# An attention-and-experts kernel: the order of all engines written out anew over cycles of four pairs

## The chip, the cores and the metric

The kernel runs on one core of one Trainium2 chip. The metric is the device time of one execution in microseconds. The engines of a core are named as in the profile: PE is the matmul array (TensorE), PEld its weight loads, DVE the vector engine, ACT the scalar engine, POOL the GpSimd engine, SP the engine whose queue issues most transfers. Each engine works through its own queue in order and waits on semaphores for the others.

## What is computed

A decaying causal attention over 8 batches x 8 heads x 576 positions of 64 values, whose output of 4608 rows of 512 goes through a mixture of 8 experts with the single best expert for each row:

```
scores = q @ k.T / 8
cum    = cumsum(log(clip(f, 1e-4, 1)))
scores = where(causal, -1e9, scores + cum[i] - cum[j])
attn   = softmax(scores);  x = attn @ v          # x: rows of 8 heads x 64
e      = argmax(x @ w_gate);  g = softmax(x @ w_gate)[e]
out    = g * (relu(x @ w1[e]) @ w2[e])           # w1: 512 x 1024, w2: 1024 x 512
```

All is float32. The term cum[i] is the same for a whole row and drops out of the softmax, so the kernel adds only -cum[j] (times 8, as the scores are scaled later).

## The kernel before

**Pairs.** Two heads make a pair, four pairs a batch, 32 pairs in all. In a pair the first 512 queries are cut into tiles t = 0 to 3 of 128 rows; tile t needs 128 (t + 1) keys. The last 64 queries of two neighbouring pairs are put together into one joint tile J, which is done with the even pair. For a pair n the steps are:

- `s_mm` (words S1, S2, S3): scores of t = 1, of t = 2 and 0, of t = 3, for head j = 0 and 1, each head into its own PSUM bank. `j_mm` (J0, J1): the two halves of the joint tile.
- `red` (r and t and j: `r10` is t = 1, j = 0) and `j_red` (q): one DVE instruction adds the decay tile, writes the scores to SBUF and gives the row's minimum (the signs are turned). `ex` (x) and `j_ex` (y): the exp on ACT with the row's sum.
- One pair later: transposes of the probabilities on PE into a bank (TA to TE for the tiles, TF to TH for J), each followed by a copy to SBUF on ACT or DVE (`cAs` is the copy of TA on ACT, `cBv` that of TB on DVE).
- Two pairs later: `av` (V0: queries 320 to 575, V1: 0 to 319) multiplies with v, and a copy (`o0s`, `o1v`) takes the result to xT. `j_place` (P) moves the joint tile's second half into place on POOL.

After the four pairs of a batch come its sums (A0 to A2), the gate logits (G, L0, L1, R), five tiles of x that are turned back, scaled on DVE and written to DRAM (F0 to F4, `fin_x`), and ten stages that choose the expert and the place of each row (the letters m e g w k s p h l b; k and b have matmuls).

**Order.** Nothing is scheduled by a program: `InOrder.pin` ties each instruction to the one before it on its engine, in the order in which the code issues it. That order stands in STEPS, a text for each of the four places of a pair in its batch, which `cycle` reads word by word. All four begin with the same words:

```python
SC = "S1 r10 r11 x10 x11 S2 r20 r00 r21 r01 S3 "
SC + """TA cAs TB cBv @0 TC cCs TD cDv @1 TE cEs !!F1 r30 r31 x20 x00 x21 x01 @2
    !!e V0 o0s x30 @3 J0 q00 q01 J1 q10 q11 @4 V1 x31 o1s !A1 !!g y0 y1 @5 @6"""
```

`!` marks a step of the batch before, `!!` of two batches before; `@0` to `@6` are slots in which loads and pieces of expert 0 are put. Pair n's loads stand ahead of its text: the decay tile of pair n + 1 (`load_d`), v of pair n, q and k of pair n + 2. On POOL `masks` copies the decay tile and adds the causal masks. A write of a tile of x to DRAM is put off by three slots (`c.later`).

**PSUM.** Eight banks. One (`ps_r`) serves the routing. Scores and J take turns in four (`ps_4`), transposes, AV and the rest in three (`ps_x`).

**Start.** Warm-up matmuls (`keep_busy`, L253) stand ahead of the first scores, and one in each slot of pairs 0 and 1. For pair 0 the decay comes from TensorE (`sel` and `cum`, a matmul of its own after each score matmul, L386), since the decay tiles are read from DRAM, where `cd` is written first; the mask-only tile `Ws[0]` is zeroed on POOL. Pair 1 and the rest use loaded decay tiles.

**End.** Expert 0 is split into two chunks of rows: the first 384 come from batches 0 to 5 and are known early. Its loads, splits into two float32r parts, first matmuls (`up`) and the turning of its rows are put into slots of the last pairs; `finish` then writes out by hand how the rest of the ups, the downs (`down`) and the routing of the last batch follow each other. Then come the second chunk of expert 0 and the experts 1 to 7, which are the same before and after.

Of the kernel before, what the change touches and what calls it, by code (L numbers as in the profile page):

```python
# [19 lines left out]
P = 128  # L20
S = 576
# [52 lines left out]
def open_pools(c, ctx, tc):  # L74
# [15 lines left out]
    c.ps_4, c.ps_x = Turns(banks[:4]), Turns(banks[4:])  # L90
# [94 lines left out]
def attention_all(c, tc, qkT, va, vb, f, wgd, x_dram, batch_done, more_consts, extra):  # L185
# [11 lines left out]
    with ExitStack() as st:  # L197
# [69 lines left out]
        NW = 9 * P  # L267
        Ws = [ap_.tile([P, 2, NW], F32, name=f"dec{i}") for i in range(2)]
# [4 lines left out]
        sel = ap_.tile([P, P], F32, name="sel")  # L273
        G.memset(sel, 0.0)
        for j in range(2):
            G.memset(sel[j * HD : j * HD + 1], 1.0)
# [13 lines left out]

        def load_d(n):
            sp_dma(Ws[n % 2][:, :, 3 * P : 7 * P],
                   cdv[n : n + 1, :, 0:512].to_broadcast([P, 2, 512]))
# [6 lines left out]
        def masks(n):  # L300
            W = Ws[n % 2]
            blk = W.rearrange("p j (a b) -> p j a b", b=P)
            m = tri.unsqueeze(1).unsqueeze(1).to_broadcast([P, 2, 2, P])
            G.tensor_copy(W[:, :, 0 : 2 * P], W[:, :, 3 * P : 5 * P])  # L304
            G.tensor_tensor(blk[:, :, 7:9], blk[:, :, 3:5], m, ALU.add)
            G.tensor_tensor(blk[:, :, 2:7:4], blk[:, :, 5:7], m, ALU.add)
# [5 lines left out]
        def decay(n, j, t):  # L312
            W = Ws[n % 2][:, j]
# [60 lines left out]
        def s_mm(n, ts):  # L374
            raw = raws[n]
            banks = [psum(c.ps_4) for _ in range(2)]
            o = 0
            for t in ts:
                w = P * (t + 1)
                for j in range(2):  # L380
                    h = slice(j * HD, (j + 1) * HD)
                    r = raw[h]
                    note(nc.tensor.matmul(banks[j][:, o : o + w], r[:, P * t : P * t + P],  # L383
                                          r[:, QW : QW + w], start=True, stop=n > 0))
                    if n == 0:
                        note(nc.tensor.matmul(banks[j][:, o : o + w], sel[h], cum[h, 0:w],  # L386
                                              start=False, stop=True))
                    got[n, j, t] = banks[j][:, o : o + w]
                o += w
# [15 lines left out]
        def j_mm(n, half):  # L405
            banks = [psum(c.ps_4) for _ in range(2)]
# [76 lines left out]
        def av(n, half):  # L483
# [4 lines left out]
            pv = psum(c.ps_x)  # L488
# [31 lines left out]
        def fin_x(b, t, scalar=False):  # L520
# [3 lines left out]
            px = psum(c.ps_s if b == B - 1 and t > 1 else fin_bank[0])  # L524
# [39 lines left out]
        def fin_logits(b, part):  # L564
            rinv = rinvs[b]
            if part == 0:
# [3 lines left out]
            pg = psum(fin_bank[0])  # L570
# [1156 lines left out]
```

## Time and profile before

| | us |
|---|---|
| median of 3 runs | 801.09 (800.36 to 802.25) |
| the profiled execution | 802.73 |
| its span, first to last instruction | 801.0 |
| PE busy in the span | 775.7 (97%) |
| DVE, ACT, POOL busy | 567.0, 496.2, 431.2 |

The span is what the trace shows; the 1.7 us around it belong to the execution's time. Busy times are sums over stages of different kinds. A matmul's end is modelled, so a busy PE is not a PE at its peak.

### The profile page before, as it was taken

To read this page: it belongs to the slowest core of one execution; us is meant where nothing else is said; L and a number is where in the kernel's file an instruction comes from. 1 tells how busy PE (TensorE), PEld (TensorE's weight loads), DVE (VectorE), ACT (ScalarE), POOL (GpSimd) and SP (SyncE) were. 2 spreads that over 40 slices of the span, in tenths; PEclk is the share of its full clock that TensorE was granted. 3 is DMA by queue.
4 is the path that set the end of the run, shared out by engine and by line. 5 is a ranking of instruction groups with operands and counts; after the bars stand their busy time and mean duration, and the time that the engine had idled before them with its cause. 6 is when DMAs were issued, how large, how long until landed. Compare 5 with 4: busy or idle time off the path is not lost.

```text
span 801.0 us, 16552 instructions
## 1 busy us (share of the span) xinstructions
PE 775.7 (97%) x5556; PEld 640.0 (80%) x5556; DVE 567.0 (71%) x1547; ACT 496.2 (62%) x1289; POOL 431.2 (54%) x602
## 2 busy tenths in 40 slices
PE   8999999999999999899999999999999999999996
PEld 6677767676777776688889899898898898998985
DVE  4676888888888888755398848758578488486630
ACT  4788887878778788545366546456365366463521
POOL 5554463636364545681567657546556475475311
PEclk9999999999999999999999999999999999999999
DMA  7987788888788877532345342363343433523300
GB/s 184 206 202 196 183 211 191 205 197 211 186 205 197 212 188 209 180 97 94 114 122 189 106 160 88 106 196 100 115 148 106 153 91 106 162 72 109 111 27 31
DMA packets 83494, 119.54 MB, mean 149 GB/s; under 512 B 9871, under 2 KB 40591, under 8 KB 83408
## 3 DMA queue, kind: packets, MB, share of 16 engines
q1 hardware_dynamic: 76272, 98.38, 46.4%
q0 software_dynamic: 6400, 19.93, 7.5%
q8 instruction: 45, 0.74, 0.4%
q14 instruction: 41, 0.34, 0.2%
q10 hardware_dynamic: 736, 0.16, 0.1%
HBM read 99.25 MB, written 20.22 MB: 149 GB/s over the span
## 4 chain that ended last, share of the span: by engine, by line
PE 84%; DVE 5%; DMA 4%; ACT 2%; issue 2%; POOL 1%; SPq 0%; ACTq 0%; POOLq 0%; DVEq 0%
PE ps L1163 25%; PE ps L1362 17%; PE ps L496 11%; PE ps L383 11%; PE ps L436 10%; PE ps L1133 3%; PE ps L411 2%; PE pr L1362 1%; PE ps L1318 1%; ACT aT L432 1%; DMA dec<-cd 1%; PE ps L557 1%; DMA va_t<-in_va 1%; DVE w1s L1267 1%; ACT row L531 1%
## 5 line engine op out<-in xcount | busy, mean ns | idle before, releaser
L369 ACT ACTIVATE sc<-sc,nmx 128x256 f32<-128x256 f32 (+3 forms) x256 | 141.2, 558 | 8.8 <-DVE nmx L366 8.8
L1163 PE MATMUL ps<-w_0w,hhw 128*128 128x512 f32 x280 | 113.0, 403 | 0.0
L1362 PE MATMUL ps<-X_0w,w1s 128*128 128x320 f32 x504 | 111.9, 309 | 0.0
L1163 PE MATMUL ps<-w_1w,hhw 128*128 128x512 f32 x280 | 110.4, 394 | 0.0
L1163 PE MATMUL ps<-w_0w,hl 128*128 128x512 f32 x280 | 110.1, 393 | 0.0
L496 PE MATMUL ps<-aT,va_t 128*64 128x256 f32 (+3 forms) x896 | 97.2, 358 | 3.9 <-PE ps L436 2.2
L383 PE MATMUL ps<-raw 64*128 64x128 f32 (+3 forms) x512 | 96.6, 457 | 3.1 <-DVE nmj L366 1.8
L496 PEld LDWEIGHTS ps<-aT,va_t 128*64 128x64 f32 x896 | 64.7, 138 | 33.2 <-PE ps L436 4.7
L366 DVE CUSTOM_DVE_ANT_0 sc<-ps,dec 128x384 f32<-128x384 f32 (+1 forms) x192 | 87.9, 508 | 4.3 <-PE ps L383 2.1
L1171 POOL DMA_INDIRECT out<-y,si_fast x37 | 37.4, 1012 | 97.6 <-ACT y L1170 89.1
L1362 PEld LDWEIGHTS ps<-X_0w,w1s 128*128 128x128 f32 x504 | 84.2, 188 | 0.2
L432 ACT COPY aT<-ps 128x256 f32<-128x256 f32 (+2 forms) x144 | 59.1, 448 | 36.6 <-PE ps L436 34.9
L1170 ACT ACTIVATE y<-ps,g_fast 128x512 f32<-128x512 f32 x37 | 25.5, 688 | 87.9 <-PE ps L1163 65.3
L1362 PE MATMUL ps<-X_1w,w1s 128*128 128x320 f32 x252 | 77.7, 308 | 0.0
L430 DVE COPY aT<-ps 128x512 f32<-128x512 f32 (+3 forms) x128 | 60.2, 503 | 19.2 <-PE ps L436 19.0
L304 POOL COPY dec<-dec 128x512 f32<-128x512 f32 x31 | 19.0, 612 | 99.5 <-DMA dec<-cd 94.3
L383 PEld LDWEIGHTS ps<-raw 64*128 64x128 f32 x512 | 56.9, 186 | 19.1 <-DVE nmj L366 2.5
L1163 PEld LDWEIGHTS ps<-w_0w,hl 128*128 128x128 f32 x280 | 52.6, 188 | 12.6
L1163 PEld LDWEIGHTS ps<-w_0w,hhw 128*128 128x128 f32 x280 | 52.5, 187 | 10.8
L1163 PEld LDWEIGHTS ps<-w_1w,hhw 128*128 128x128 f32 x280 | 52.7, 188 | 10.4
L1362 PE MATMUL ps<-xa,w1s 128*128 128x320 f32 x336 | 58.4, 309 | 1.0 <-ACT u L1391 1.0
L1267 DVE TENSOR_TENSOR w1s<-w1r,w1s 128x1024 fp32r<-128x1024 f32 (+1 forms) x42 | 52.8, 1269 | 7.8 <-ACT w1s L1261 7.8
(263 smaller groups left out, 1799.2 us busy)
## 6 DMA issues: line engine op xcount, KB each, us to landing
dec<-cd SPq DMA_DIRECT2D x31, 512.0 KB, 5.6
w1r<-in_w SPq DMA_DIRECT2D x112, 128.0 KB, 3.0
w<-in_w SPq DMA_DIRECT2D x28, 512.0 KB, 4.7
raw<-in_qkT SPq DMA_DIRECT2D x64, 160.0 KB, 5.6
raw<-in_qkT SPq DMA_DIRECT2D x64, 144.0 KB, 5.1
decj<-cd SPq DMA_DIRECT2D x32, 288.0 KB, 4.9
va_t<-in_va SPq DMA_DIRECT2D x32, 256.0 KB, 6.4
x_dram<-row SPq DMA_DIRECT2D x32, 256.0 KB, 3.9
```

The source lines that it names most:

```text
L366: V.tensor_tensor_reduce(dst, src, m, -0.125, init, ALU.add, ALU.min, out)
L369: nc.scalar.activation(x, x, AF.Exp, bias=nmx, scale=-1.0, accum_out=acc)
L383: note(nc.tensor.matmul(banks[j][:, o : o + w], r[:, P * t : P * t + P], r[:, QW : QW + w], start=True, stop=n > 0))
L430: V.tensor_copy(dst, src)
L432: nc.scalar.copy(dst, src)
L436: note(nc.tensor.transpose(out.bitcast(F32R), words, c.identr))
L496: c.last_av = note(nc.tensor.matmul(pv[j * HD : (j + 1) * HD, q0 - qa : qb - qa], l, r, start=(blk == 0), stop=(blk == nb - 1),))
L1163: c.note(nc.tensor.matmul(py, rows(hi_, ft), w[wi], start=(ft + k == 0), stop=(ft == FT - 1 and k == 2),))
L1170: nc.scalar.activation(y, py, AF.Copy, scale=g[:, s : s + 1])
L1171: nc.gpsimd.indirect_dma_start(out=self.out, out_offset=bass.IndirectOffsetOnAxis(ap=si[:, s : s + 1], axis=0), in_=y, in_offset=None, bou ...
L1267: (eng or self.nc.vector).tensor_tensor(lo, raw, hi.bitcast(F32), ALU.subtract)
L1362: self.nc.tensor.matmul(bank[:, 0:HN], w[:, wi, mat, kt], x[xi][:, kt, :], start=start and k == 0, stop=k == 5, skip_group_check=True,)
```

## The change

The order is one text from the first pair to the last: FIRST for pairs 0 to 3, STEPS for a cycle of four pairs (used for pairs 4 to 27), LAST for pairs 28 to 31 and all of expert 0's first chunk. Each word that needs PSUM names its banks (`S2:ta` is the bank t for head 0 and a for head 1), out of seven that all steps share; transposes, AV and scores of neighbouring pairs are mixed more freely, loads (D, DJ, LV, LR), masks (M, MJ) and writes of x (W0 to W4) are words of their own. Copies move between ACT and DVE. Slots, `c.later`, `early_tasks` and `finish` go.

In the start, four warm-up pairs instead of eight and none later; pairs 0 and 1 share the mask-only tile and get their decay by matmuls (words Z, `z_mm`; `sel` holds -8 in one row for each of them, so `cum` is not multiplied by -8 ahead of the scan); pair 1's decay tile is not loaded. The zeroing of `Ws[0]` moves to DVE, the multiplication by -8 for the DRAM copy to POOL.

In the end, w1 loads and splits (`wl`, `ws`), w2 loads and splits (`vl`, `vs`), row fetches and turns (`ef`, `et`, `ee`), ups and downs (`u`, `d`) are words of LAST.

```diff
-    c.ps_4, c.ps_x = Turns(banks[:4]), Turns(banks[4:])
+    c.bank = dict(zip("abcdtvm", banks))
...
-        step(lambda: keep_busy(8))
+        step(lambda: keep_busy(4))
         V.memset(ones, 1.0)
+        NW = 9 * P
+        Ws = [ap_.tile([P, 2, NW], F32, name=f"dec{i}") for i in range(2)]
+        V.memset(Ws[0], 0.0)
         V.tensor_scalar(fr, fr, 1.0e-4, 1.0, ALU.max, ALU.min)
         nc.scalar.activation(fl, fr, AF.Ln)
         pin(nc.scalar.activation(warm, fr[0:1, 0:1], AF.Exp))
-        V.tensor_scalar(fl, fl, -8.0, None, ALU.mult)
         V.tensor_tensor_scan(cum, ones, fl, 0.0, ALU.mult, ALU.add)
-        sp_dma(cd, cum)
...
-        G.memset(Ws[0], 0.0)
-        for j in range(2):
-            for k in (2, 6, 7, 8):
-                G.tensor_copy(Ws[0][:, j, k * P : k * P + P], tri)
+        G.tensor_copy(blocks(Ws[0])[:, :, 7:9], tri4)
+        G.tensor_copy(blocks(Ws[0])[:, :, 2:7:4], tri4)
...
+        G.tensor_scalar(fl, cum, -8.0, None, ALU.mult)
+        sp_dma(cd, fl)
...
+        def dec(n):
+            return Ws[(n + 1) % 2 if n > 1 else 0]
...
+                    note(nc.tensor.matmul(banks[j][:, o : o + w], r[:, P * t : P * t + P],
+                                          r[:, QW : QW + w], start=True, stop=n > 1))
+                    got[n, j, t] = banks[j][:, o : o + w]
+                if n < 2 and len(ts) > 1:
+                    z_mm(n, (t,))
...
+        def z_mm(n, ts):
+            for t in ts:
+                for j in range(2):
+                    h = slice(j * HD, (j + 1) * HD)
+                    note(nc.tensor.matmul(got[n, j, t], sel[h, n], cum[h, 0 : P * (t + 1)],
+                                          start=False, stop=True))
...
         STEPS = [
+            """J0:dt q01 D J1:cb q00 q11 S3:mv A0 y1 LR q10 S2:ta A1 S1:bd r30 V1:c r21 r31 r20 y0
+               r01 r00 r10 x30 r11 e M V0:m o1s TE:a F3:v A2 x00 TA:t x31 o0s TC:c W0 cEs LV cAv
+               F4:d cCs TD:b x01 k cDs x11 s TB:v x10 cBv x21 x20""",
+            """S2:ma r01 S1:bc r00 r10 r20 r21 S3:dt r30 TA:v x00 r31 TG:b D cAs LV p TF:m r11 x20
+               V0:a x31 cFs TH:d cGs TC:t TD:v M DJ o0v cHv cCv LR x30 TB:c F1:m g TE:d cBs l MJ
+               x11 V1:b cEs x21 cDs o1v P x01 x10""",
+            """S3:tm r30 S2:ad r31 D r20 G:bc x30 r01 S1:tm r21 x31 w r00 r11 x20 V1:v r10 J0:ma
+               J1:db TD:t q01 M q00 cDs x00 q11 L1:a TC:c LV q10 y1 F2:m h o1s LR TB:b TE:a cBs
+               TA:t L0:d V0:m cAs y0 x21 o0s cEv x10 cCv x11 W3 x01""",
+            """S1:ta S2:bv r11 R S3:md r21 r10 r01 V1:a r30 TE:c o1v TA:t TB:m r00 x11 r20 TG:v D
+               r31 LR cAv cEs b DJ F0:c x00 TC:d TH:a cGs TD:v cBs x01 cCs TF:t V0:m W4 x30 cFs cDv
+               W2 x20 m x31 W1 cHv M x21 MJ o0v P LV x10""",
         ]
+        FIRST = """
+            0.LV 0.S3:bd 0.S1:am 0.Z1 0.S2:vt -1.LC 0.r10 0.r20 0.x10 0.Z3 -1.LG 0.r01 0.r30 0.r11
+            0.r00 0.r21 0.x01 0.x11 0.x00 -1.DJ 0.J0:tb 0.x30 -1.MJ 0.x21 0.x20 0.r31 1.D 0.x31
+            0.J1:ac 0.q01 0.q00 0.q11 0.y1 -1.MC 0.q10 0.y0 1.S2:vd -1.MC 0.LR 1.r20 1.S3:bm
...
+        LAST = """
...
+            32.cCs 32.V0:b 33.V1:t 34.ee1 34.ws2 32.A0 32.cAv 32.o1s 32.o0s 34.ws1 33.V0:d 33.A1
+            33.o1v 33.o0s 34.et2:b 34.et0:c 34.G7:va 32.s 34.ee2 34.ee0 32.F2:m 33.A2 34.F37v:t
+            32.W4 32.p 34.F27s:d 34.L07:v 34.vl1 34.u1:b 34.W37 32.W2 32.l 34.vs0 32.w 34.vl2
+            34.u3:t 34.F07v:m 34.L17:c 34.W07 34.F17v:b 34.u5:v 34.W27 34.F47s:m 32.h 34.u4:d 34.m7
+            34.u0:v 34.e7 34.g7 34.vs1 34.u2:c 34.d10:v 34.d20:m 34.k7 34.d00:t 34.d21 34.s7 34.vl3
+            34.W17 34.W47 34.vs2 32.F3:a 32.b 34.h7 34.d01 34.l7 34.d11 32.F1:c 34.vs3 34.d02 32.W3
+            34.b7 34.ix 34.u6:c 32.W1 34.ef3 34.u7:b 34.d22 34.d12 34.ef4 34.d03 34.d23 34.et3:d
+            34.d13 34.ee3 34.et4:m 34.ee4
+            """
```

## Rows read from the trace of the kernel before

**Rows 1.** The page's first part (busy us, share of the span, number of instructions) and, of its second, the weight loads' busy share in tenths in 40 equal slices of the span.

```profile
PE 775.7 (97%) x5556; PEld 640.0 (80%) x5556; DVE 567.0 (71%) x1547; ACT 496.2 (62%) x1289; POOL 431.2 (54%) x602
...
PEld 6677767676777776688889899898898898998985
```

**Rows 2.** Busy time of each engine by stage (length; then busy us and number of instructions; granted PE clock, DMA share, GB/s): the start, pairs 0 to 3, pairs 4 to 27, pair 28 to the second chunk of expert 0, the rest.

```profile
0.00:9.54 9.54, 6.62 (x16) 5.07 (x16) 4.58 (x9) 3.65 (x5) 8.42 (x27) 1.00 0.59 177
9.54:46.63 37.09, 35.45 (x286) 26.01 (x285) 23.93 (x96) 27.30 (x90) 18.60 (x38) 1.00 0.90 207
46.63:290.14 243.51, 236.71 (x2232) 173.83 (x2229) 202.30 (x754) 196.70 (x630) 122.94 (x232) 1.00 0.81 198
290.14:389.08 98.94, 92.91 (x730) 73.42 (x728) 65.30 (x225) 59.47 (x177) 50.83 (x78) 0.98 0.50 147
389.08:801.00 411.92, 404.04 (x2301) 361.70 (x2299) 270.88 (x464) 209.10 (x389) 230.44 (x227) 1.00 0.37 115
```

**Rows 3.** The same for one cycle of four pairs in the middle.

```profile
145.38:186.11 40.73, 39.63 (x380) 29.16 (x377) 34.66 (x129) 32.88 (x106) 21.60 (x43) 1.00 0.82 202
```

**Rows 4.** PE's AV matmuls of two widths in that cycle (mean ns behind the busy us).

```profile
L496 PE MATMUL ps<-aT,va_t 128*64 128x192 f32 x32 | 4.1, 326 | 0.0
...
L496 PE MATMUL ps<-aT,va_t 128*64 128x64 f32 x20 | 1.4, 220 | 0.0
```

**Rows 5.** PE in order of time in that cycle (start, us from first start to last modelled end, line, what, how many). L496 is AV, L411 J, L557 the gate, L383 the scores, L436 transposes.

```profile
150.90 1.84 PE L496 MATMUL ps<-aT,va_t 128*64 128x256 f32 x16 [0.26 <-PE ps L436]
...
152.79 1.20 PE L411 MATMUL ps<-raw 64*64 64x288 f32 x16
153.92 1.20 PE L496 MATMUL ps<-aT,va_t 128*64 128x320 f32 x12
155.05 1.18 PE L557 MATMUL ps<-xT,wg 128*32 128x512 f32 x16
156.15 2.90 PE L383 MATMUL ps<-raw 64*128 64x256 f32 x16
158.98 0.53 PE L436 MATMUL ps<-identr,sc_Jw 128*128 128x128 f32 x4
...
160.82 0.54 PE L436 MATMUL ps<-identr,sc_02w 128*128 128x128 f32 x4
...
161.86 0.29 PE L436 MATMUL ps<-identr,sc_Jw 128*68 128x128 f32 x2
...
163.78 1.84 PE L496 MATMUL ps<-aT,va_t 128*64 128x256 f32 x16 [0.20 <-PE ps L436]
...
166.65 0.70 PE L383 MATMUL ps<-raw 64*128 64x256 f32 x4
```

**Rows 6.** Who waited for whom in that cycle: us in total, times, longest (from the lists of PEld, DVE and ACT).

```profile
PEld ps L436 <- ACT sc L369: 3.0, 4, 0.8
...
DVE aT L430 <- PE ps L436: 2.3, 6, 0.5
...
ACT aT L432 <- PE ps L436: 4.6, 8, 1.0
ACT xT L432 <- PE ps L496: 2.2, 4, 0.9
```

**Rows 7.** Copies by shape: on DVE and ACT in that cycle, and (third row) the one AV copy on DVE, in the end of the attention part.

```profile
L430 DVE COPY aT<-ps 128x512 f32<-128x512 f32 x6 | 4.1, 691 | 1.9 <-PE ps L436 1.9
...
L430 DVE COPY aT<-ps 128x384 f32<-128x384 f32 x4 | 2.2, 553 | 0.4 <-PE ps L436 0.4
...
L430 DVE COPY xT<-ps 128x320 f32<-128x320 f32 x1 | 0.5, 492 | 1.8 <-PE ps L496 1.8
...
L432 ACT COPY aT<-ps 128x512 f32<-128x512 f32 x6 | 3.6, 593 | 2.5 <-PE ps L436 2.5
...
L432 ACT COPY xT<-ps 128x320 f32<-128x320 f32 x4 | 1.7, 416 | 0.8 <-PE ps L496 0.8
```

**Rows 8.** All engines in order of time in the head: POOL zeroes the first mask tile, SP writes cd, POOL masks the joint decay tile, DVE's first reduction of pair 1.

```profile
1.08 2.02 POOL L277 MEMSET dec<- 128x2304 f32 x1
...
7.40 0.37 SPq L223 DMA_DIRECT2D cd<-aT  x1
...
15.04 0.45 POOL L309 TENSOR_TENSOR decj<-decj,trij 128x128 f32<-128x128 f32 x1 [5.57 <-DMA decj<-cd]
...
21.05 0.42 DVE L366 CUSTOM_DVE_ANT_1 sc<-ps,dec 128x256 f32<-128x256 f32 x1 [2.42 <-POOL dec L305]
```

**Rows 9.** The ups of expert 0's first chunk, by line, and (second row) the longest pieces of the chain that ended last: 66 down matmuls of a later expert.

```profile
L1133 PE MATMUL ps<-xa,w 128*128 128x384 f32 x96 | 19.0, 344 | 0.4 <-ACT xa L1103 0.3
...
454.96 15.46 PE ps L1163 x66
```

**Rows 10.** PE in order of time: warm-up matmuls in the head (L253), then scores after a wait and an AV first part in the end of the attention part.

```profile
2.92 6.69 PE L253 MATMUL pr<-gT 128*128 128x256 f32 x16 [2.92 <-DVE gT L248]
...
14.16 1.99 PE L253 MATMUL pr<-gT 128*128 128x256 f32 x8
...
322.98 3.80 PE L383 MATMUL ps<-raw 64*128 64x256 f32 x16 [1.81 <-DVE nmj L366]
...
332.49 2.79 PE L496 MATMUL ps<-aT,va_t 128*64 128x256 f32 x16
```

**Rows 11.** Busy time of each engine and granted PE clock in the ten us around that AV.

```profile
330.00:340.00 10.00, 8.76 (x72) 6.53 (x74) 6.03 (x24) 5.64 (x18) 4.16 (x6) 0.83 0.61 192
```

More of the change, by code (lines that the diff above doesn't have):

```diff
@@ L371, in attention_all, with s_mm @@
         got = {}
-        def s_mm(n, ts):
+        def s_mm(n, ts, pools):
             raw = raws[n]
-            banks = [psum(c.ps_4) for _ in range(2)]
+            banks = [psum(k) for k in pools]
             o = 0
@@ L401, in ex, with j_mm @@
                   ssums[b][:, t, 2 * p + j : 2 * p + j + 1])
-        def j_mm(n, half):
-            banks = [psum(c.ps_4) for _ in range(2)]
+        def j_mm(n, half, pools):
+            banks = [psum(k) for k in pools]
             o = QW + half * JW
@@ L698, in slot @@
-        def slot(n, i):
-            for x in c.later:
-                x[0] -= 1
-            while c.later and c.later[0][0] <= 0:
-                c.later.pop(0)[1]()
-            if i in (2, 4) and 2 <= n < 5:
-                next(c.more, None)
-            if n < 2:
-                step(lambda: keep_busy(1))
-            for f in tasks.pop((n, i), []):
-                step(f)
-            if (n, i) == (NP, 0):
-                scores.close()
-            for f in extra(n, i):
-                step(f)
@@ L721, in attention_all, with begin @@
+        loads = {
+            "D": lambda n: load_d(n + 1), "DJ": lambda n: load_dj(n + 1), "LV": load_v,
+            "LR": lambda n: load_pair(n + 2), "M": lambda n: masks(n + 1),
+            "MJ": lambda n: masks_j(), "LC": lambda n: late_consts(), "LG": lambda n: load_gate(),
+            "MC": lambda n: next(c.more, None),
+        }
+        more = extra()
+        def begin(n):
+            if n in begun:
+                return
+            begun.add(n)
             b, p = divmod(n, NPAIR)
-            if n < NP and p == 0:
+            if p == 0:
@@ new lines, in last @@
+        def last(w, at):
+            k = w[0]
+            if k in "FGLW" or w[1:] == "7" and k in "megkshlb":
+                b = B - 1
+                if k == "F":
+                    fin_x(b, int(w[1]), w[3] == "s", *at)
+                elif k in "GLW":
+                    of_batch(b, w[:-1], at)
+                else:
+                    for x in {"g": "gw", "s": "sp"}.get(k, k):
+                        stages[b]["megwksphlb".index(x)]()
+            else:
+                k = w.rstrip("0123456789")
+                more[k](*map(int, w[len(k):]), *at)
@@ new lines, in go @@
+        def go(n, w):
+            if w == "vs0":
+                scores.close()
+            step(lambda: do(n, w))
+            order.pin()
+        order = InOrder(tc)
+        c.note = note
+        order.pin()
+        for w in FIRST.split():
+            go(*(lambda n, x: (int(n), x))(*w.split(".")))
+        for n in range(NPAIR, NP - NPAIR):
+            for w in STEPS[n % NPAIR].split():
+                go(n, w)
+        todo = [(int(n), x) for n, x in (w.split(".") for w in LAST.split())]
@@ L754, in run, with rest @@
+        while todo[0][1] != "vs3":
+            go(*todo.pop(0))
+    def rest():
+        for n, w in todo:
+            go(n, w)
     def run(f):
@@ L756, in run @@
         order.pin()
-    return run, todo
+    return run, rest
 def setup_routing(c, tc, B):
@@ L1419, in seven, with run @@
         self.ends = [end, lambda: relu(g, 0, 1), lambda: (rest(p5, 1, 1), rest(g, 0, 1))]
-    def run(self, run, tasks):
+    def run(self, run, rest):
         c, tc = self.c, self.tc
@@ L1437, in run @@
             self.w2pools.append(w2b)
-            self.finish(run, tasks)
+            rest()
             c.note = lambda r: r
```

365 lines of the change are left out of this document (149 added, 216 removed).

## The prediction

> **What bounds the kernel now.** I read the page's shares first: TensorE 97% busy over the span, but its weight loads at 6 or 7 tenths in each of the first 20 slices and at 8 or 9 in nearly all later ones [rows 1]. So the first 400 us are not as full as the 97% says. Next the table by stage [rows 2]: a head of 9.54 us before the first scores and 37.09 us for pairs 0 to 3, then 243.51 us for pairs 4 to 27, 98.94 us from pair 28 to the second chunk of expert 0, and 411.92 us of experts, which the diff leaves alone. What can change is the first 389 us.
>
> The middle repeats every four pairs; 145.38 to 186.11 is one cycle, 40.73 us [rows 3]. In it PE shows 39.63 busy, DVE 34.66, ACT 32.88. But a matmul row carries a tail that overlaps the next matmul: 64 columns take 220 ns and 192 take 326 [rows 4], which is 0.83 ns a column and a fixed 0.17 us. A drained array between two groups therefore shows as busy. The honest measure is from the start of a group to the start of the next [rows 5]: a J group 1.13 us, AV in one piece 2.87 (163.78 to 166.65), AV in two 1.89 and 1.13, the gate 1.10, twelve transposes 1.04, so 0.087 each. Scores: 1280 columns in two passes, the two heads side by side, are 2.13 us by the slope and 2.3 with the 0.17 that J (0.96 by the slope, 1.13 seen) pays for starting a group; the trace has 2.83. Sum per cycle: scores 4 x 2.3 = 9.2, AV 2 x 2.87 + 2 x 3.02 = 11.8, J 2.3, gate 1.1, 100 transposes of probabilities 8.7, 20 of x 1.7, logits, rank and table 1.2: 36.0 us. So PE waits about 4.7 us in each cycle, and no engine is full: PE 36.0, DVE 34.7, ACT 32.9 of 40.73. The named waits [rows 6] say why: PE's first transposes wait for the last exps (3.0 us), ACT's and DVE's copies wait for those transposes (4.6 and 2.3), ACT waits for AV (2.2). Three in-order engines take turns at the seam of each pair.
>
> **The change, part by part.**
>
> *Cycle of four pairs (six cycles).* Work per cycle hardly moves. DVE gives up two 512 copies and one C/D set (2 x 0.69 + 0.55 + some 0.3) and takes four AV copies (0.49, and about 0.42 for the narrower): 34.7 becomes 34.3. ACT takes what DVE gives and becomes about 33.3, by its own rows of 0.59 and 0.41 [rows 7]. PE groups change array shape 17 times a cycle before and, counted off the new text, 20 times: 3 x 0.17 = +0.5, so 36.5. POOL and SP keep their instructions. Every decay tile still has at least a pair and a half, some 14 us, between the last reader of its buffer and its first use, and q, k and v are loaded as far ahead as before, so I put no price on SP's new order; uncovered, a late decay tile costs what it cost pair 1 (2.4 us, below). The x writes move from a fixed delay to named places up to ten pieces behind their row, so SP, whose loads queue behind a write, should wait less for DVE.
>
> What the new order does at the seam: the transposes of pair n-1 come after all of pair n's scores, and mostly behind one AV half. In the first step, J, S3, S2, S1, V1, V0 (8 us by the rows above) stand ahead of TE, whose input is ACT's last exp of the pair before. That wait of 3.0 us and the two copy waits behind it lose their cause. Walking that step by the rows: q01 to q10 release banks d, t, b, c by 3.0 us, S2 and S1 use t, a, b, d from 2.0 to 3.3, V1 takes c at 3.6, TE at 6.6 just after DVE has emptied bank a; PE is next able to start pair 1's S2 at about 9.3, when ACT has copied TE out of bank a. Its own groups need 8.7. So I find about 0.6 us of wait in that pair, where the trace has 1.2 a pair now. The hand-over from engine to engine is not in such a walk. I take 37.9 us a cycle: the floor of 36.5 plus 0.35 a pair. Bounds: 36.5 (none left) and 40.6 (nothing gained). Middle: 6 x (40.6 - 37.9) = **16 us off**, bounds 25 and 0.
>
> *Head.* The zeroing of the first mask tile goes from POOL (2.02 us [rows 8]) to DVE, ahead of the clip, and -8 moves behind the scan to POOL; the cd write should go from 7.40 to about 8.7, and decj with it from 15.04 to about 16.4, just before the first J reduction of old (16.9). So nothing is lost there, and pair 0's scores can start when four instead of eight warm-up pairs are over. Pair 1 no longer waits for its decay tile: its first reduction waited 2.42 us for POOL's masks and came at 21.05; after pair 0's J reductions it can start at about 18.6. The 16 extra matmuls (pair 1's cum terms, 2.1 us) fall where PE idles. Then three pairs at about 0.5 us less each: **4 us off**, bounds 6 and 0 (if the clock falls, below).
>
> *End.* The new text runs all attention first (pairs 28 to 31, AV of 30 and 31) and then the gate of the last batch with ups and downs woven in. By the rows: attention there is scores 9.2, J 2.3, 120 transposes 10.4, AV 6 x 2.9 = 17.4, seven x tiles 2.4, gate, logits, rank, table, three turns 3.4: 45 us. Behind it: eight ups 19.0, 72 down matmuls at 0.234 = 16.8 [rows 9], gate 1.1, eight x tiles 2.7, the rest 1.8: 41 us. So 86 of 98.94 are work. DVE and ACT carry about 42 us each in the attention part, so PE will not be dense there, and the last pair's exps, transposes and AV form a chain with only three turns as filler; the last turn ends 0.3 us ahead of the ups that read it (a copy 0.59 and a subtraction 0.69 stand between; before, 2.8 us of downs hid them). From rank to table the last batch's route has five quarters of downs (6 x 0.234 each) and two x tiles as cover on PE, 7.7 us, and the fetch of its last two tiles has an up and four quarters, 8 us; I cost both at nothing, and a few us of PE idle if they run over. I take 90: **9 us off**, bounds 13 and 2.
>
> Sum: 16 + 4 + 9 = 29 us. The profiled execution took 802.73 with a span of 801.0; the median of the runs is 801.09, so 29 off the median gives **772 us**.
>
> **The clock, and a rule of the Trainium skill.** The warm-up matmuls, 256 columns each, took 6.69 us for 16 from 2.92 on and 1.99 for 8 at 14.16: half clock (1.2 GHz) first and full clock (2.4 GHz) later. And after PE idled for 1.8 us before 322.98 [rows 10], the window 330 to 340 shows a granted clock of 0.83 on average [rows 11]: one AV first part (16 matmuls) took 2.79 us where it takes 1.84, and the stretch cost about 1.5 us in all. The change halves the first warm-up and drops the later ones; I count no loss for it, and 3 us (two such stretches) as its bound. The Trainium skill, "TensorE: Matmul & The Clock Gate", section Part 1, says that an idle array falls back to half clock; by it the bank waits of pairs 0 and 1 would bring one or two such stretches, and the head's gain would be 1 to 2 us and not 4. The sum would be 775 by that and is 772 by the rows; both lie in the forecast's own range.
>
> **Rivals.**
>
> *The weave gets nearly everything.* Cycle 36.8, end 87, head 6 off: 23 + 12 + 6 = 41, so 760. For it: DVE and ACT fit under PE. Against: three engines above 90% at once in strict order.
>
> *The middle gains little.* The waits come back as bank waits: before, scores had four banks of their own, now 75 allocations a cycle share seven. A transposed bank is held until its copy, and copies stand in ACT's order behind exps that wait for DVE. Cycle 39.8: 5 + 9 + 4 = 18, so 783. DMA pulls the same way: 0.82 busy in a cycle of 40.73 is 0.88 at 37.9; the head ran at 0.90 [rows 2, 3], so it should hold, but landings will be longer.
>
> *Slower.* The same ring closes on itself: a late copy holds a score bank, the scores start late, their reductions and exps start late, and the next copy behind them is later still, with no empty bank to take up the delay. It decides once a cycle takes over 42.8 (2.2 x 6 = the 13 that head and end give). At 43.5, i.e. 1.75 us of wait per pair over the floor where now it is 1.2: -17 + 13, so 805. Against it: in the step that I walked the bank is free before or just as it is wanted.
>
> *No change* (the order of before was already all that the banks allow, and head and end give nothing): 801.
>
> **How the numbers follow.** My forecast (765 to 779) 0.50, nearly everything 0.13, little in the middle 0.22, no change 0.03, slower 0.12. Two runs apart by less than 0.2% (1.6 us) can't be told apart. Faster 0.85, same 0.03, slower 0.12. The range 755 to 792 holds the first three cases but for their outer edges, and leaves out the slower one; the forecast's own range is 765 to 779.
>
> **What would show it.** Right: a cycle of four pairs in the middle of 37 to 39 us; weight loads of PE there busy near 77%; the wait of transposes for exps and of copies for transposes gone from the list of waits; pair 1's first reduction before 19.5; the second chunk of expert 0 starting near 360. Wrong: a new wait of PE on ACT's copies of aT or xT ahead of scores, half clock in more than one stretch, DMA landings that someone waits for in the middle, or a cycle over 40. If the end is where I erred, PE will show gaps between the last scores and the gate.

## The result, and the profile after

The changed kernel takes 772.4 us (median; 770.4 to 773.3), the kernel before took 801.7 us beside it: a ratio of 0.962 with a 95% interval of 0.957 to 0.967. The forecast was 772 us. The sum came out; most of the reason given for its largest term did not, as the experiments show. One execution below, of the kernel with the fetches moved, took 1011 us at a granted clock of 0.655; it is left out of that kernel's time.

The page's first part and weight-load line of the changed kernel (they answer to [rows 1]):

```profile
PE 748.0 (97%) x5536; PEld 612.9 (79%) x5536; DVE 561.8 (73%) x1553; ACT 486.9 (63%) x1269; POOL 427.6 (55%) x593
...
PEld 3676777767676767887898898898998998988985
```

The table by stage, with the same columns as [rows 2]; the sixth row is one cycle of four pairs (against [rows 3]), the last a stretch of the head. The profiled execution took 773.26 us, its span is 771.5.

```profile
0.00:6.58 6.58, 3.65 (x8) 2.52 (x9) 4.74 (x8) 1.49 (x2) 4.55 (x24) 1.00 0.65 177
6.58:44.17 37.58, 32.38 (x273) 21.61 (x273) 26.94 (x101) 27.61 (x90) 16.74 (x31) 0.95 0.76 197
44.17:268.65 224.49, 220.81 (x2233) 157.98 (x2230) 196.09 (x756) 192.18 (x627) 123.18 (x232) 1.00 0.85 216
268.65:358.28 89.63, 86.75 (x731) 68.85 (x728) 62.84 (x226) 57.23 (x166) 51.28 (x80) 1.00 0.55 159
358.28:771.50 413.22, 404.45 (x2300) 361.89 (x2300) 271.25 (x465) 208.36 (x388) 231.89 (x228) 1.00 0.37 115
154.96:192.60 37.65, 36.62 (x372) 26.23 (x370) 33.95 (x128) 31.86 (x106) 21.44 (x42) 1.00 0.82 216
20.12:23.53 3.41, 3.41 (x12) 1.68 (x10) 1.97 (x10) 2.82 (x8) 3.13 (x9) 0.50 0.97 306
```

Stage by stage: up to pair 4, 46.63 became 44.17 (-2.5); pairs 4 to 27, 243.51 became 224.49 (-19.0, 37.4 a cycle); pair 28 to the second chunk of expert 0, 98.94 became 89.63 (-9.3); the rest, 411.92 became 413.22 (+1.3). Together -29.5.

The waits in that cycle (us in total, times, longest) against [rows 6]:

```profile
ACT aT L447 <- PE ps L451: 2.9, 4, 1.5
...
PEld ps L451 <- DVE nmx L375: 1.3, 2, 0.8
...
PEld ps L511 <- DVE nmx L375: 1.1, 2, 0.8
...
DVE sc L375 <- DMA dec<-cd: 0.9, 1, 0.9
```

The rows of transposes waiting for exps (3.0) and of DVE's copies waiting for transposes (2.3) are gone, as forecast; ACT's copies still wait 2.9 us for transposes, where it was 4.6. That looks like a proof of the forecast's mechanism. It isn't.

### The profile page after: what moved, and what is told of

Read it like the earlier page. It is cut to its first block, busy times and chain, and to the rows that moved or that the text cites. A ratio compares the mean times of both kernels' runs of the same rounds, so it can differ in the third digit from the quotient of the medians.

```text
span 771.5 us, 16307 instructions
## 1 busy us (share of the span) xinstructions
PE 748.0 (97%) x5536; PEld 612.9 (79%) x5536; DVE 561.8 (73%) x1553; ACT 486.9 (63%) x1269; POOL 427.6 (55%) x593
## 4 chain that ended last, share of the span: by engine, by line
PE 77%; DVE 11%; issue 3%; DMA 3%; ACT 3%; POOL 1%; SPq 1%; ACTq 0%; POOLq 0%; DVEq 0%
PE ps L1198 26%; PE ps L1385 18%; PE ps L511 8%; PE ps L451 8%; PE ps L391 8%; DVE sc L375 4%; PE ps L1168 2%; PE ps L426 2%; DMA decj<-cd 2%; PE pr L1385 1%; PE ps L1341 1%; PE ps L568 1%; ACT sc L378 1%; ACT aT L447 1%; DVE w1s L1290 1%
## 5 line engine op out<-in xcount | busy, mean ns | idle before, releaser
L378 ACT ACTIVATE sc<-sc,nmx 128x384 f32<-128x384 f32 (+3 forms) x256 | 143.5, 573 | 8.8 <-DVE nmx L375 8.8
L375 DVE CUSTOM_DVE_ANT_0 sc<-ps,dec 128x512 f32<-128x512 f32 (+2 forms) x192 | 88.9, 506 | 9.9 <-ACT sc L378 3.4
L511 PE MATMUL ps<-aT,va_t 128*64 128x256 f32 (+3 forms) x896 | 95.2, 355 | 0.0
L511 PEld LDWEIGHTS ps<-aT,va_t 128*64 128x64 f32 x896 | 58.2, 136 | 35.6 <-DVE nmx L375 6.7
L391 PE MATMUL ps<-raw 64*128 64x256 f32 (+3 forms) x512 | 82.7, 452 | 2.4 <-DVE nmj L375 2.4
L447 ACT COPY aT<-ps 128x512 f32<-128x512 f32 (+4 forms) x170 | 70.8, 453 | 20.9 <-PE ps L451 19.3
L391 PEld LDWEIGHTS ps<-raw 64*128 64x128 f32 x512 | 43.0, 187 | 26.4 <-issue 6.8
L1198 PEld LDWEIGHTS ps<-w_1w,hhw 128*128 128x128 f32 x280 | 52.7, 188 | 10.4
L1427 POOL TENSOR_TENSOR u<-u,u 128x320 f32<-128x320 f32 x28 | 24.6, 877 | 61.5 <-DVE u L1425 61.4
L1284 ACT CAST w1s<-w1r 128x1024 fp32r<-128x1024 f32 (+1 forms) x56 | 52.1, 944 | 7.8 <-POOL w1r L1270 7.8
```

Of the source, the lines that this page charges most:

```text
L375: V.tensor_tensor_reduce(dst, src, m, -0.125, init, ALU.add, ALU.min, out)
L378: nc.scalar.activation(x, x, AF.Exp, bias=nmx, scale=-1.0, accum_out=acc)
L447: nc.scalar.copy(dst, src)
L511: c.last_av = note(nc.tensor.matmul(pv[j * HD : (j + 1) * HD, q0 - qa : qb - qa], l, r, start=(blk == 0), stop=(blk == nb - 1),))
L1198: c.note(nc.tensor.matmul(py, rows(hi_, ft), w[wi], start=(ft + k == 0), stop=(ft == FT - 1 and k == 2),))
L1284: self.nc.scalar.copy(t[:, 0], raw)
```

## Experiments on the middle

In the changed kernel the lines are 391 for scores, 426 for J, 451 for transposes, 511 for AV, 568 for the gate, 375 for reductions, 378 for exps, 445 and 447 for copies on DVE and ACT. Pairs 4 to 27 can be given another text and the start and end left alone. To compare such texts I add up, over the middle, the time from the start of each PE matmul to the start of the next, by the kind of the first: waits then count for the kind that they follow or split, and modelled ends don't matter. It runs from the first score matmul of pair 4 to that of pair 28 (in the changed kernel one J group, 1.1 us, falls ahead of it; rank and table, 3 to 5 us, are left out).

| pairs 4 to 27, us | whole | scores | transposes | AV | J | gate | time, median |
|---|---|---|---|---|---|---|---|
| before | 243.5 | 70.1 | 78.7 | 70.6 | 13.6 | 6.6 | 801 to 803 |
| old order, banks 4 + 3 | 244.2 | 69.8 | 79.6 | 70.6 | 13.6 | 6.6 | 791.9 |
| old order, seven shared | 227.8 | 68.0 | 65.6 | 70.6 | 13.6 | 6.6 | 774.3 |
| old order, only transposes and AV share | 238.8 | 74.5 | 66.0 | 73.8 | 13.6 | 7.5 | 786.6 |
| old order, six shared | 240.1 | 71.6 | 70.9 | 70.6 | 13.6 | 10.4 | 787.5 |
| AV first, banks 4 + 3 | 267.3 | 75.1 | 76.7 | 74.8 | 30.2 | 6.6 | 816.2 |
| AV first, seven shared | 259.0 | 87.5 | 66.2 | 73.1 | 15.0 | 13.9 | 809.2 |
| changed kernel | 223.4 | 58.0 | 69.7 | 71.5 | 12.5 | 6.6 | 772.4 |
| new order, old engines for copies | 235.6 | 65.9 | 73.8 | 71.5 | 13.3 | 6.6 | 784.8 |
| new order, banks by rule | 227.8 | 58.3 | 70.5 | 71.5 | 16.3 | 6.6 | 776.4 |

**The old order put back.**

```diff
-  """J0:dt q01 D J1:cb q00 q11 S3:mv A0 y1 LR q10 S2:ta A1 S1:bd r30 V1:c ...
+  """D M LV LR W0 A0 S1:ab r10 r11 x10 x11 S2:cd r20 r00 r21 r01 S3:ab TA:t cAs TB:v cBv
+     TC:m cCs TD:t cDv TE:v cEs F1:m r30 r31 x20 x00 x21 x01 e V0:t o0s x30 J0:cd ...
```

> The changed kernel, with the order of before (and its banks, four for scores and three for the rest, and its engines for the copies) put back in pairs 4 to 27 alone; start and end stay new. Theory, that the order in the middle gives two thirds of the gain: the cycle of four pairs goes from 37.65 back to about 40.6 us, six cycles give 18 to 19 us, so about 791 us, and the waits of transposes for exps (3.0 us a cycle before) and of copies for transposes (4.6 and 2.3) are back. Rival, that the gain came with start and end, or from a state that the start leaves behind (loads further ahead, a clock that holds): 772 to 780 us, with a cycle under 39.

791.9 us, ratio 0.988 (0.985 to 0.990), middle 244.2. So the text of the middle is worth 19.5 us and the rest of the change about 10. But this text holds three things: an order, a choice of banks and a choice of engines. ("Banks 4 + 3" is not quite a split by purpose: in odd pairs two tiles of transposes, TB and TC, take score banks, here as in the kernel before.)

**The banks alone.** The same text, each step taking the bank that has been free longest:

```diff
-  S1:ab r10 r11 x10 x11 S2:cd r20 r00 r21 r01 S3:ab TA:t cAs TB:v cBv TC:m cCs TD:t cDv TE:v
+  each :xy replaced by the bank (or two) of a, b, c, d, t, v, m that was emptied first
```

> As the run with the old order in pairs 4 to 27, but each step takes the bank of the seven that has been free longest, so only the split into four and three banks is gone. Theory, that the order and not the sharing of banks gives the gain: within 3 us of that run, some 788 to 794 us, cycle about 40.3. Rival, that three banks for transposes and AV were too few and that sharing seven is what lets PE run ahead: 775 to 782 us, cycle 38 to 39, with the copies' and AV's waits gone.

774.3 us, ratio 0.965 (0.963 to 0.967). The theory fell, the rival holds: the order of before, word for word, with its banks shared, gets 17.6 of the 19.5 us. PE in order of time, two neighbouring groups, first with banks 4 + 3, then with seven shared (start, us, line, how many):

```profile
123.35 2.90 PE L391 MATMUL ps<-raw 64*128 64x256 f32 x16
126.18 0.53 PE L451 MATMUL ps<-identr,sc_03w 128*128 128x128 f32 x4
126.55 0.50 PE L451 MATMUL ps<-identr,sc_13w 128*128 128x128 f32 x4
126.89 0.50 PE L451 MATMUL ps<-identr,sc_02w 128*128 128x128 f32 x4
127.39 0.54 PE L451 MATMUL ps<-identr,sc_12w 128*128 128x128 f32 x4
127.84 0.37 PE L451 MATMUL ps<-identr,sc_01w 128*128 128x128 f32 x2
...
128.82 1.84 PE L511 MATMUL ps<-aT,va_t 128*64 128x256 f32 x16
```

```profile
118.47 0.54 PE L451 MATMUL ps<-identr,sc_03w 128*128 128x128 f32 x4
118.85 0.50 PE L451 MATMUL ps<-identr,sc_13w 128*128 128x128 f32 x4
119.18 0.50 PE L451 MATMUL ps<-identr,sc_02w 128*128 128x128 f32 x4
119.52 0.50 PE L451 MATMUL ps<-identr,sc_12w 128*128 128x128 f32 x4
119.86 0.33 PE L451 MATMUL ps<-identr,sc_01w 128*128 128x128 f32 x2
...
120.63 1.84 PE L511 MATMUL ps<-aT,va_t 128*64 128x256 f32 x16
```

From the first transpose to AV it is 2.64 us above and 2.16 below, for the same 24 transposes. Above, the fourth tile starts 0.50 after the third (126.89 to 127.39) and the next 0.45 later, where it is 0.34 below: each waits for the copy out of the bank three turns back (ACT's copy out of the first tile's bank runs from 126.75 to 127.34, DVE's out of the second's from 127.09 to 127.78). All in all the transposes of the middle fall from 79.6 to 65.6 us.

The Trainium skill, "Perfetto Trace Analysis", section Optimizing Tensor Performance, has independent groups of matmuls rotate through PSUM banks, so that the copy out of one overlaps the next group; and its section Optimization Strategy takes the same gap, repeated, as a sign that SBUF or PSUM may be short for the next tile. Both runs agree with it: the transposes take 14 us less by banks alone.

**Half of the sharing.** `S` and `J` keep a, b, c, d; the rest takes any bank.

> The old order in pairs 4 to 27, with only half of the sharing: scores and joint tiles keep their four banks, transposes, AV and the rest take whichever of all seven has been free longest. It divides the 17 us that sharing gave. Theory now, that the larger part is S3 waiting for the reductions r10 and r11 of the banks that S1 took (a score group is 2.83 us long with four banks and 2.36 with seven, 24 times 0.47 = 11 us): this run keeps that wait and gains only the transposes' part, 5 to 7 us, so about 785 us, and its score groups stay at 2.8 us. Rival, that three banks for transposes and AV are the tight ones: 776 to 779 us, with score groups near 2.4 since the pair before ends earlier.

786.6 us, ratio 0.982 (0.979 to 0.985). The number of the theory came, its reason did not. The transposes gained as much as with all seven shared (66.0), and scores and AV gave more than half of it back (74.5 and 73.8 for 69.8 and 70.6), since the scores' four banks are now also lent out. AV's part is the scores' wait too: it all stands at the 18 places where scores follow AV (2.7 us with banks 4 + 3, 6.0 here). With all seven shared a score group is still 68.0 / 24 = 2.83 us long on average. So it was never S3 that made up most of the 17 us, but the transposes, and these only as long as the scores may step aside in turn.

The list of PEld's waits in one cycle, with banks 4 + 3 and then in this run (us, times, longest):

```profile
PEld ps L451 <- ACT sc L378: 3.0, 4, 0.8
PEld ps L451 <- ACT aT L447: 0.9, 3, 0.5
PEld ps L511 <- PE ps L451: 0.9, 3, 0.4
```

```profile
PEld ps L451 <- ACT sc L378: 3.0, 4, 0.8
...
PEld ps L391 <- DVE nmj L375: 0.5, 1, 0.5
```

The large wait, on which the forecast rested, is the same to the digit in a kernel whose transposes run 13.6 us faster. It costs next to nothing, as PE's own rows show. The seam on PE, with banks 4 + 3 (the first row is the last score matmul alone):

```profile
125.66 0.59 PE L391 MATMUL ps<-raw 64*128 64x512 f32 x1
126.18 0.53 PE L451 MATMUL ps<-identr,sc_03w 128*128 128x128 f32 x4
```

The first transpose starts 0.52 us after the last score matmul. It does so at each of the 24 seams of the middle, in the kernel before and in all four kernels with the old order and the transposes behind the scores, whatever their banks. That matmul's 512 columns take 0.43 of it by the slope of [rows 4]. The weight load of that transpose, with banks 4 + 3 and with seven shared:

```profile
126.18 0.39 PEld L451 LDWEIGHTS ps<-identr,sc_03w 128*128 128x128 f32 x4 [0.76 <-ACT sc L378]
```

```profile
118.47 0.39 PEld L451 LDWEIGHTS ps<-identr,sc_03w 128*128 128x128 f32 x4 [0.76 <-issue]
```

The same idle time is put down to ACT's exp in one kernel and to nobody in the other. The weight loads stand idle while the array finishes, and the list names whoever signalled last. The wait of 0.9 for ACT's copies of aT, a small row under it, was a real one.

**One bank less.**

> The old order in pairs 4 to 27 with sharing, but over six banks and the seventh unused. Theory, that S3 needs a third pair of banks and the transposes need three or four for a while, but not at once: between the shared seven (774 us) and the split seven (792 us), nearer the first: 776 to 782 us, so that six shared banks beat seven split. Rival, that every bank counts: 788 us or more.

787.5 us, ratio 0.983 (0.981 to 0.985): neither, but nearer the rival. The seventh bank is worth 13 us here, and six shared still beat seven split by 4.

**Work for PE at the seam.** If PE did wait there for exps, a piece of AV in between should hide it:

```diff
-  S3:ab TA:t cAs TB:v cBv TC:m cCs ... V0:t o0s x30
+  S3:ab V0:t o0s TA:v cAs TB:m cBv TC:t cCs ... x30
```

> As the run with the old order and the old banks in pairs 4 to 27, with one step moved: the first AV half (V0 and its copy) stands right behind the scores, ahead of the transposes, in each pair. Theory, that the wait at the seam is lack of work on PE between the scores and the last exps of the pair before: the wait of transposes for exps falls from 3.0 us a cycle to under 0.8, the cycle from 40.6 to about 39, so 781 to 784 us. Rival, that the work is only moved from one wait to another (the later exps and copies then come 1.9 us later and AV's second half waits for them): cycle 40 or more, 788 us or more.

(In the third pair of a cycle F4 moves ahead with it.) 816.2 us, ratio 1.017 (1.015 to 1.019): 24 us slower than without the step, far beyond what even the rival named. In this kernel's order of time on PE, the joint tile:

```profile
139.19 0.71 PE L426 MATMUL ps<-raw 64*64 64x288 f32 x8
140.65 1.32 PE L426 MATMUL ps<-raw 64*64 64x288 f32 x8 [0.74 <-DVE nmx L375]
```

Its second half waits for a bank that r30 or r31 must empty; these stand in DVE's order behind the transposes' copies, and those now behind AV. J takes 30.2 us instead of 13.6. So the same step once more with shared banks:

> The old order with the first AV half ahead of the transposes, as in the run that took 816 us, but with the bank of the seven that has been free longest. Theory, that its loss came from the four score banks (the joint tile waited for the last reductions, which stand behind the copies of the transposes that AV had put off): the joint group falls from 2.7 to about 1.2 us and the time to 774 to 780 us. Rival, that the loss is the order of ACT's and DVE's own queues (the AV copy ahead of the transposes' copies, DVE waiting 9.5 us a cycle for transposes): over 795 us.

809.2 us, ratio 1.012 (1.009 to 1.015): J is mended (15.0), and scores take 87.5 and the gate 13.9. The rival holds. The waits of DVE and ACT in a cycle of it:

```profile
DVE aT L445 <- PE ps L451: 8.1, 4, 2.9
```

```profile
ACT xT L447 <- PE ps L511: 7.0, 4, 2.6
```

The first instruction in the queues of two engines waits until AV or the transposes are over, and the reductions and exps behind it come late for the next scores. Work put at PE's seam starved the engines that feed PE.

**The engines of the copies.** Fifteen copies a cycle back to the engine of before, in the new order:

```diff
-  ... TA:t x31 o0s TC:c W0 cEs LV cAv ... V0:a ... DJ o0v ... V1:b ... o1v
+  ... TA:t x31 o0s TC:c W0 cEs LV cAs ... V0:a ... DJ o0s ... V1:b ... o1s
```

> The changed kernel, new order, with 15 copies a cycle given back to the engine that did them before (all AV copies to ACT; of the transposes' copies some each way). Theory, that the choice of engine is second to the order: within 0.5 us a cycle, so 770 to 776 us. Rival, that DVE and ACT are close enough to their limit (34 and 32 of 37.65 us) for the choice to be part of the gain: 1 to 2 us a cycle, 778 to 785 us.

784.8 us, ratio 0.979 (0.976 to 0.982): the rival holds. With the old engines the new order is 10 us worse than the old order with shared banks, and its scores take 65.9 us for 58.0. New in the list of weight loads are scores behind ACT's copies of xT (1.2 us a cycle) and of aT (0.7). The banks of this text were named for the new engines; how much of the 12 us is theirs was not tried.

**Names or rule.** The new order and engines with the bank that is free longest:

> The changed kernel with new order and new engines, but in pairs 4 to 27 the banks named in the text are replaced by the one that has been free longest. Theory, that it matters that seven are shared and not which is named: 771 to 775 us, cycle 37.3 to 38.3. Rival, that the names were chosen to fit the copies' times: 778 us or more.

776.4 us, ratio 0.968 (0.966 to 0.971), between the two: the banks named by hand are worth about 4 us over a plain rule, nearly all at J (16.3 for 12.5).

What isn't settled: the new order with banks 4 + 3 can't be written, as its first step puts S3, S2 and S1, two banks each, ahead of the first of their reductions. So a pure worth of the new order doesn't exist; on top of sharing, order, engines and named banks together give 3 us (227.8 to 224.5).

## Experiments on the start and the end

The head of the changed kernel, all engines in order of time (against [rows 8]):

```profile
3.92 1.98 DVE L260 MEMSET dec<- 128x2304 f32 x1 [0.43 <-issue]
...
6.05 0.83 DVE L261 TENSOR_SCALAR aT<-aT 128x576 f32<-128x576 f32 x1
...
9.09 1.68 POOL L290 TENSOR_SCALAR aT<-aT 128x576 f32<-128x576 f32 x1 [1.74 <-DVE aT L264]
...
10.79 0.37 SPq L223 DMA_DIRECT2D cd<-aT  x1
...
19.21 0.46 DVE L375 CUSTOM_DVE_ANT_0 sc_J<-ps,decj 128x288 f32<-128x288 f32 x1 [4.43 <-DMA decj<-cd]
...
20.84 0.55 DVE L375 CUSTOM_DVE_ANT_0 sc<-ps,dec 128x384 f32<-128x384 f32 x1
```

The clip waits for 1.98 us of zeroing, cd for 1.68 us of multiplication, so the joint tile's reduction comes at 19.21. PE in order of time shows which waits the end of the attention part has (L991 the last route's table, L1168 the second chunk's ups, L1341 expert 1's first turn):

```profile
343.96 0.69 PE L991 MATMUL pr<-Rr,Ar 128*128 128x240 bf16 x5 [0.86 <-DVE Ar L984]
...
358.28 0.50 PE L1168 MATMUL ps<-xb,w 128*128 128x256 f32 x2 [1.68 <-ACT xb L1138]
...
366.00 0.53 PE L1341 MATMUL ps<-identr,xg 128*128 128x128 f32 x4 [1.21 <-DMA xg<-x_dram,gi_fast]
```

**Both mended.**

```diff
-        V.memset(Ws[0], 0.0)
+        G.memset(Ws[0], 0.0)
...
         V.tensor_tensor_scan(cum, ones, fl, 0.0, ALU.mult, ALU.add)
+        V.tensor_scalar(fl, cum, -8.0, None, ALU.mult)
+        sp_dma(cd, fl)
...
-        G.tensor_scalar(fl, cum, -8.0, None, ALU.mult)
-        sp_dma(cd, fl)
...
-  32.F3:a 32.b 34.h7 34.d01 34.l7 34.d11 32.F1:c 34.vs3 34.d02 32.W3 34.b7 34.ix 34.u6:c 32.W1
-  34.ef3 34.u7:b 34.d22 34.d12 34.ef4 34.d03 34.d23 34.et3:d 34.d13 34.ee3 34.et4:m 34.ee4
+  32.F3:a 32.F1:c 32.b 34.h7 34.d01 34.l7 34.d11 34.vs3 34.d02 32.W3 32.W1 34.b7 34.ix 34.u6:c
+  34.ef3 34.ef4 34.u7:b 34.d22 34.d12 34.d03 34.et3:d 34.d23 34.ee3 34.et4:t 34.d13 34.ee4
```

> The changed kernel with two mendings outside the middle. Head: the first mask tile is zeroed on POOL again, and -8 is multiplied on DVE right behind the scan, so the clip no longer waits for a 1.98 us zeroing and cd no longer for a 1.68 us multiplication. End: the tile of x that the fetch of expert 0's last rows waits for (batch 6, t = 1) is made and written ahead of the last route, both fetches stand together, and the two last turns stand one down quarter earlier. Theory: cd is written near 7.7 instead of 10.8, the first joint reduction comes near 16 instead of 19.2, pair 4 starts 3 us earlier; the fetch of the last rows starts near 347 - 3 instead of 349.7, and the wait of 1.9 us ahead of the second chunk's ups goes: 767 to 769 us. Rival, that the head is bound by something later (loads of pairs 2 and 3, the half clock after the gap) and the end by the route's own chain: 771 to 773 us.

> The changed kernel once more, beside the run with its head and end mended, so that the two stand against the same runs of before: 771 to 774 us; all its stages as in its first trace.

771.2 against 772.4 us, ratios 0.963 (0.961 to 0.966) for both: no difference that can be told. And yet, in the traces, cd is written at 7.52 and not at 10.79, the joint reduction comes at 16.33, and the second chunk of expert 0 starts at 351.14 and not at 358.28: 7.1 us are won by then, and the span is 2.9 us shorter. (Some 2 of the 7.1 are the clock: this execution kept the full clock in the head, and the next kernel, with the same head and a stretch at half clock there, starts that chunk at 352.94.) Where 4.2 us went, PE and POOL of the mended kernel show:

```profile
352.39 1.00 POOL L1206 DMA_INDIRECT out<-y,si_early  x1 [2.50 <-ACT y L1205]
355.86 0.98 POOL L1206 DMA_INDIRECT out<-y,si_early  x1 [2.48 <-DMA out<-y,si_early]
357.14 1.00 POOL L1119 DMA_INDIRECT xg<-x_dram,gi_fast  x1 [0.30 <-issue]
...
360.62 0.72 PE L1341 MATMUL ps<-identr,xg 128*128 128x128 f32 x4 [3.32 <-DMA xg<-x_dram,gi_fast]
361.14 2.89 PE L1168 MATMUL ps<-xb,w 128*128 128x256 f32 x12
```

Each scatter of expert 0's rows waits for the one before to land, one every 3.5 us, and the fetch of expert 1's rows stands behind all three on POOL's queue. PE waits 3.32 us, and the twelve ups behind that take 2.89 us where they take 1.67 at full clock; the granted clock is 0.50 (1.2 GHz) from 359.60 to 366.42.

**The fetches moved ahead of the scatters.**

```diff
-  34.ef3 34.ef4 34.u7:b
+  34.ef3 34.ef4 34.en3 34.en4 34.u7:b                    # en: self.fetch(1, m)
...
-                0: [S(self.begin_t), fetch(1, 3), fetch(1, 4)], 1: [fetch(1, 2), fetch(1, 0)],
+                0: [S(self.begin_t)], 1: [fetch(1, 2), fetch(1, 0)],
```

> The run with head and end mended, and one step more: the fetches of expert 1's first two row tiles stand right behind those of expert 0's last two on POOL's queue, ahead of expert 0's three scatters (in the run before they stood behind them, and a scatter starts only when the one before has landed, every 3.5 us). Theory, that the 7 us won up to the second chunk were given back there (a wait of 3.3 us for these rows instead of 1.2, and half clock behind it): the wait at expert 1's first turn is gone, the ups behind it stay at full clock, 764 to 767 us. Rival, that the experts are held by something else that keeps its own time (their weights' loads or POOL's sums): 769 to 772 us, with a new wait later.

764.4 us, ratio 0.954 (0.952 to 0.956): the theory holds, and this kernel beats both. The fetches of expert 1's first two tiles are issued at 345.05 and 346.31, and PE shows no wait:

```profile
352.94 6.17 PE L1168 MATMUL ps<-xb,w 128*128 128x256 f32 x48
358.94 0.46 PE L1341 MATMUL ps<-identr,xg 128*128 128x128 f32 x4
359.23 1.67 PE L1168 MATMUL ps<-xb,w 128*128 128x256 f32 x12
```

**Warm-ups in the head's gaps.**

```diff
-  0.x00 -1.DJ 0.J0:tb ...  1.r20 1.S3:bm
+  0.x00 -1.DJ -1.K7 0.J0:tb ...  1.r20 -1.K4 1.S3:bm     # K7: keep_busy(7)
```

> The best run so far (765.1 us) with eleven warm-up matmuls put into PE's two gaps of the head: seven ahead of pair 0's joint scores (PE waited 1.82 us there), four ahead of pair 1's last scores. Theory, that what is left of the head's loss is the half clock that follows those gaps: the half-clock stretch (3.5 us at 0.50, so 1.7 us of loss) does not come, pair 4 starts near 40.8 instead of 42.6, 763 to 764.5 us. Rival, that the stretch comes in some executions only, so that nothing is seen in the median, or that the warm-ups hold the scores up: 764.5 to 767 us.

769.7 us, ratio 0.959 (0.957 to 0.961): about 5 us worse, beyond what even the rival named. PE's order of time:

```profile
12.09 3.29 PE L253 MATMUL pr<-gT 128*128 128x256 f32 x14
15.31 1.20 PE L426 MATMUL ps<-raw 64*64 64x288 f32 x16
```

The clock stayed full, but each of these float32 matmuls shows as two rows, so the seven are 14 and take 3.29 us in a gap of 1.82: J starts at 15.31 instead of 13.94. Pair 4's first scores come at 44.19 instead of 42.56; the rest of the loss lies in later stages, about 1 us or less in each, and its cause is open; the six executions spread from 766.5 to 770.7. Whether fewer warm-ups would pay was not tried.

## Why the prediction was right, and where it wasn't

Middle, head, end and the rest were forecast at 16, 4, 9 and 0 us off and came as 19.0, 2.5, 9.3 and -1.3. The errors cancel in the sum, so that the total was met within 1 us is in part luck.

**PE's floor and the missing 4.7 us a cycle: right.** Start-to-start lengths said that PE had 36.0 us of work in a cycle that showed 39.63 busy. The changed kernel runs a cycle in 37.4, its scores in 58.0 / 24 = 2.4 us (2.3 forecast).

**Middle, 16 off: 19.0, for another reason.** The step that failed is "the named waits say why". I took the wait of the transposes for exps as the seam's price and the order as its cure. That row had next to no cost (0.52 us at every seam, 0.43 of it the last matmul's columns), work put at the seam (AV ahead of the transposes) makes the kernel slower than before, and the old order with shared banks does nearly all. That 16 came near 19 is owed to the floor, which was read rightly; the 0.35 us of wait a pair above it came from a walk through the waits that failed. The 4.7 us a cycle, 28 in the middle, sat inside the groups: transposes had 14.8 over their floor (78.7 less 734 x 0.087) and scores 14.9 (70.1 less 24 x 2.3). Of the first, 14.0 went with the sharing of banks; of the second, 1.8 went with it and 10 with the new order, its engines and its banks together (with the old engines only 2.1 of these 10), while the transposes rose again from 65.6 to 69.7. Both lengths stand in the prediction (0.087 a transpose, 2.83 for 2.3 a score group), and the question what is waited for inside a group was not asked.

**The bank rivals: the wrong way round.** "Now 75 allocations share seven" was set down as a danger at 0.22 and 0.12. A split of four and three was the bound: the transposes ran out of banks (79.6 us, and 66.0 where they may take any), and the scores in turn once only theirs were lent out (74.5 for 69.8); with all seven shared both come down (65.6 and 68.0). What the rival said of a late copy that holds a bank fits the new order with the old engines, whose scores take 7.9 us longer.

**The engines of the copies: costed as balance, worth 12 us.** DVE 33.95 and ACT 31.86 a cycle agree with 34.3 and 33.3. But a busy sum doesn't show when a bank comes free. (The 12 us are those of the new order with its named banks.)

**DMA: right in the main.** 0.82 busy and 216 GB/s in a cycle. But one wait of DVE for a decay tile, 0.9 us, is there, and a landing that someone waits for in the middle was set down as a sign of being wrong.

**Head, 4 off: 2.5.** Two terms failed. The cd write was put at 8.7 and came at 10.79, as the multiplication on POOL takes 1.68 us where DVE takes 0.46 in the mended kernel; so the joint reduction came at 19.21, not 16.9, and pair 1's first reduction at 20.84, not 18.6. And the clock, for which no loss was counted: after PE idled 2.18 us ahead of 19.73 the granted clock was 0.50 (1.2 GHz) from 20.12 to 23.53, a loss of 1.7 us. The Trainium skill, "TensorE: Matmul & The Clock Gate", section Part 1, which the prediction weighed against its rows, was right on this in this trace: one such stretch came. But five of the ten traces with this head stay at full clock there, one of them (only transposes and AV share) after PE idled 1.89 us ahead of 19.43. In that one and in the one with seven shared, both with the old order behind the head, pair 4's scores start at 42.83 and 42.20, and before at 46.63. So at full clock the head gives about the 4 us of the forecast, late joint reduction and all; what made up for the late write is open.

**End, 9 off: 9.3.** The wait that the forecast warned of, last turn to ups, is there (1.9 us), and so is the table's (0.9).

**The rest, 0: +1.3.** Not foreseen. PE waits 1.2 us for the rows of expert 1, whose fetch stands behind the scatters, where it had no such wait before; that eats what an earlier end wins: the mended end gained nothing until it was moved.

**Signs.** Cycle 37 to 39 and the second chunk near 360: right. Pair 1's first reduction before 19.5: wrong, 20.84. Waits of transposes for exps and of copies for transposes gone: the first yes, the second on DVE but not on ACT (2.9 us). Weight loads near 77% of a cycle: wrong, 26.23 of 37.65 is 70%, less than the 72% of before, in a faster kernel. The weight loads of the scores alone fell from 42.4 to 31.7 us over the middle at the same number (384), so this row seems to hold waits too, and shrinks with them.

## What to carry to other kernels

When PE is the bound, compare groups of equal matmuls from start to start, and look for the bank that a slow group waits for before reading the list of waits: a wait there may only be the engine in front finishing its work. Ask of each set of buffers whether it runs dry while another has some to spare; sharing was worth 17.6 us here, and the new order with its engines and named banks 2 to 3 more on top. And before a stage's gain is booked, follow it to the next queue that keeps its own time.

## What was not expected of the hardware

The granted clock in the head differs between executions of the same program text up to pair 3. Of ten traces with this head, five show 0.83 as the mean between 15 and 25 us (one stretch at 0.50) and five show 1.00. Why is open. Where the half-clock stretch fell on PE's own gaps (banks 4 + 3 with the old order) pair 2's scores still start at 24.9; where it came behind them (the changed kernel) they start at 26.9.

The same clip of 128 x 576 on DVE takes 0.83 us in the changed kernel, where POOL copies beside it, and 0.47 in the mended one, where POOL is at other work.
